# Attention, gated MLP and softplus MLP on one core: Strassen's seven products for the last matrix product of three token groups, and shorter chains of small vector instructions

## The chip, the cores and the metric

The kernel runs on one core of a Trainium2 chip. The metric is the device time of one execution in microseconds (us). Time before: a median of 699.16 us over 3 runs (698.99 to 699.61). The profile that is read below comes from one more execution, which took 698.44 us, with a span of 696.5 us from its first to its last instruction.

## The reference, cut to what matters

```python
# q, k, v: (4, 8, 576, 64) fp32; heads 0-3 see a window of 32 keys, heads 4-7 every 4th key of 128
attn = softmax(where(mask, q @ k.T / 8, -1e9))        # per head
x = (attn @ v) laid out as (2304, 512)                # tokens x (heads * 64)
h = x @ moe_w_in                                      # (2304, 1024)
solu = h * softmax(h)
ln = (solu - mean(solu)) / sqrt(var(solu) + 1e-6) * g_ln
y = ln @ moe_w_out                                    # (2304, 512)
h2 = y @ moe2_w_in                                    # (2304, 2048)
g = maximum(h2, 0) + log1p(exp(-abs(h2)))             # softplus
out = g @ moe2_w_out                                  # (2304, 512) fp32
```

## The kernel before, in words

All matrix products of the MLPs are made with fp16 operands that stand for fp32 ones: each operand is split into a high and a low half (`... h` and `... l` operations: a cast on VectorE or ScalarE, then a subtraction on VectorE), and each product is three matmuls (high by high, high by low, low by high) that add up in PSUM. The weights come in as fp32, are scaled by a power of two that is found on the chip (`weights`: sum of squares on ScalarE, a sum over the partitions by a matmul with a tile of ones, then a chain of small VectorE instructions, `scale_of` and what follows it), and are split into the tile `W`, which holds all four matrices for the rest of the run.

The 2304 tokens go through in 28 attention pairs, 18 tiles of 128 tokens for the first MLP's first product, softmax and norm (`m1`), and 9 groups of 256 tokens, numbered 0 to 8, for everything after that. The norm needs 1/sqrt(var + eps); it is made on VectorE from an integer guess and Newton steps (the chain `m1k`, 9 instructions of one column, and `m1x`).

Of a group, `y` = ln @ w_out comes first, then, for 8 pairs of 128 hidden columns (p = 0 to 7), the hidden product, the softplus on ScalarE (`sp`), the split of its result g into halves (`gh`, `gl`), and the output product (`o`), which adds into the PSUM tile `ps_w`. One `o` of one p is 2 token halves x 2 hidden halves x 3 = 12 matmuls, with g as the stationary operand (128x128) and 512 columns of w2_out moving.

Groups 5 and 6, and 7 and 8, go in twos (`TWINS`, functions `twin_weights`, `y_twin`, `mlp2_twin`): their hidden product is made by Strassen's method in Winograd's form, with seven products of blocks (`P5.0.1` to `P7.3.7`: twin, quarter of the hidden columns, product) in place of eight. That takes sums of weight blocks (`tw..`), sums of y blocks (`yt..`) and sums of the products out of PSUM (`U`, `C`), all on VectorE. The output products `o` are still plain ones in all nine groups.

The order of the work is a list of numbers, `ORDER`: one sequence of operations over all engines, which was found by a search outside the kernel; each engine runs its own operations in that order. For an operation that either VectorE or ScalarE could do, the number also says which one does it. `SLOTS` says which buffer each tile takes. Negative numbers are matmuls without use (`eye` by `eye`, 512 columns), which stand where TensorE was expected to have nothing to do; they are called fillers below. There are 142.

Of the kernel before, what the change touches and what calls it, by code (L numbers as in the profile page):

```python
# [1749 lines left out]
```

## Time and profile before

| what | value |
|---|---|
| median of 3 runs | 699.16 us |
| profiled execution: time, span | 698.44 us, 696.5 us |
| PE (TensorE matmul) busy | 675.2 us, 97% of the span, 5223 records |
| DVE (VectorE) busy | 556.0 us, 80% |
| ACT (ScalarE) busy | 480.9 us, 69%, of which 55.2 us are 43 loads of an activation table |
| DMA moved | 89.8 MB |
| mean granted TensorE clock | 0.988 of full speed |

The busy time of PE includes the fillers, so a busy PE is not yet a useful PE. A matmul's duration in the trace (379 ns for 512 columns) is longer than the distance to the next one, because they overlap in the array; distances between starts tell the rate. VectorE's records overlap a little too. Shares over the whole span mix stages with different limits, so the rows below are read by stage.

### The profile page before, as it was taken

Reading aid. Unit: us, or ns where it says so; the run is one execution under the profiler, and the core shown is the slowest. Engines: PE = TensorE matmul, PEld = TensorE weight load, DVE = VectorE, ACT = ScalarE, POOL = GpSimd, SP = SyncE. Lnnn points to the kernel's source line nnn. Section 1 sums busy time; section 2 is a strip of 40 time slices with the busy share of each in tenths; the row PEclk is TensorE's granted clock in tenths of the full one; section 3 lists DMA queues with packets and bytes.
Section 4 is the critical chain, followed back from the end, with each engine's and each line's share of the span. In section 5 each row is a group of like instructions: output and inputs, shape, how many; then the busy total and the mean of one; then the engine's idle time right before and its main releaser. Section 6 shows DMA issues by size and latency. Waiting matters only on the chain.

```text
span 696.5 us, 14184 instructions
## 1 busy us (share of the span) xinstructions
PE 675.2 (97%) x5223; PEld 463.9 (67%) x5223; DVE 556.0 (80%) x1619; ACT 480.9 (69%) x1015; POOL 3.5 (1%) x22
## 2 busy tenths in 40 slices
PE   7999699999999999999999999999999999999997
PEld 4665547766765588688667668666776668676653
DVE  4999999999999968788889899887887768544233
ACT  4889998999998776987799797976364632322312
POOL 2000000000000000000000000000000000000000
PEclk9999689999999999999999999999999999999999
DMA  9889987669876558989887887652012110000001
GB/s 266 247 233 259 225 225 193 162 170 188 184 147 164 146 176 185 200 162 157 158 152 153 153 162 136 116 113 43 1 31 62 31 31 1 1 32 31 1 1 60
DMA packets 186773, 89.80 MB, mean 129 GB/s; under 512 B 157000, under 2 KB 174416, under 8 KB 186704
## 3 DMA queue, kind: packets, MB, share of 16 engines
...
## 4 chain that ended last, share of the span: by engine, by line
PE 69%; DVE 12%; DMA 10%; ACT 4%; issue 3%; SPq 1%; ACTq 0%; DVEq 0%
PE ps_w L552 31%; PE bank L552 26%; PE bank L1550 11%; DMA xd<-x 2%; DVE E L543 2%; DMA E<-in_v_dram 2%; DMA qT<-qk 1%; DMA pT<-p 1%; DVE W L543 1%; PE bank L558 1%; DVE s L1122 1%; DMA W<-in_moe_w_out_dram 1%; ACT E L534 1%; DMA rv<-in_v_dram 1%; DMA rq<-in_q_dram 1%
## 5 line engine op out<-in xcount | busy, mean ns | idle before, releaser
L552 PE MATMUL ps_w<-W,g 128*128 128x512 f16 x864 | 194.3, 379 | 0.0
L552 PEld LDWEIGHTS <-W 128*128 128x128 f16 x1824 | 176.5, 98 | 23.3 <-DMA lnT<-hl 0.7
L552 PEld LDWEIGHTS <-g 128*128 128x128 f16 x864 | 83.6, 98 | 91.4
L552 PE MATMUL bank<-y,W 128*128 128x256 f16 x960 | 109.9, 273 | 0.0
L552 PE MATMUL ps_w<-W,xr 128*128 128x512 f16 x432 | 99.5, 382 | 1.0 <-ACT xr L534 1.0
L552 PE MATMUL bank<-lnT,W 128*128 128x256 f16 x864 | 98.7, 273 | 0.2 <-DMA lnT<-hl 0.2
L552 PEld LDWEIGHTS <-xr 128*128 128x128 f16 x432 | 42.1, 99 | 46.9 <-ACT xr L534 1.5
L543 DVE SCALAR_TENSOR_TENSOR g<-r,KR,g 128x512 f16<-128x512 f32 x68 | 50.3, 744 | 15.2 <-ACT g L534 14.2
L1718 ACT ACT_TABLE_LOAD x43 | 55.2, 1283 | 0.7
L1550 PEld LDWEIGHTS <-W 128*128 128x128 f16 x480 | 47.0, 98 | 8.4
L534 ACT ACTIVATE E<-E 128x768 f32<-128x768 f32 (+3 forms) x51 | 37.9, 744 | 15.7 <-DVE E L543 8.8
L534 ACT ACTIVATE s<-s 96x128 f32<-96x128 f32 (+3 forms) x144 | 43.5, 374 | 2.4 <-DVE st L538 1.2
L1122 DVE CUSTOM_DVE_ANT_0 s<-bank,band,bsc 96x128 f32<-96x128 f32 (+3 forms) x144 | 38.9, 324 | 3.9 <-PE bank L552 3.6
L534 ACT ACTIVATE r<-bank,invC 128x512 f32<-128x512 f32 x40 | 27.2, 685 | 16.4 <-PE bank L552 15.5
L534 ACT ACTIVATE r<-r,invT 128x512 f32<-128x512 f32 x21 | 14.6, 714 | 32.5 <-DVE r L546 32.4
L534 ACT ACTIVATE xf<-bank,rs 80x64 f32<-80x64 f32 (+1 forms) x128 | 29.3, 314 | 7.2 <-DVE rs L549 4.8
L552 PE MATMUL ps_w<-eye 128*128 128x512 bf16 x108 | 31.4, 407 | 0.7 <-DVE e L543 0.7
L534 ACT ACTIVATE g<-r,KR 128x512 f16<-128x512 f32 x35 | 24.9, 715 | 6.6 <-PE ps_w L552 6.3
L552 PEld LDWEIGHTS <-pT 128*96 128x96 f16 (+3 forms) x432 | 23.1, 123 | 6.9 <-issue 1.5
L543 DVE SCALAR_TENSOR_TENSOR E<-E 128x512 int32<-128x512 int32 x40 | 27.1, 683 | 0.1
L552 PEld LDWEIGHTS <-eye 128*128 128x128 bf16 (+2 forms) x162 | 16.5, 111 | 15.8 <-POOL eye L611 4.0
L534 ACT ACTIVATE hl<-e,st 128x1024 f16<-128x1024 f32 x18 | 22.3, 1242 | 5.4 <-DMA lnT<-hl 3.2
...
## 6 DMA issues: line engine op xcount, KB each, us to landing
...
```

The costliest lines, as they stand in the source:

```text
L534: pin(nc.scalar.activation(out=out, in_=in_, func=func, **kw))
L543: pin(nc.vector.scalar_tensor_tensor(out=out, in0=in0, scalar=s, in1=in1, op0=op0, op1=op1, **kw))
L552: pin(nc.tensor.matmul(out, l, r, start=start, stop=stop))
L558: pin(nc.tensor.transpose(out, in_, eye32[:in_.shape[0], :in_.shape[0]]))
L1122: pin(nc.vector.tensor_tensor_reduce(out=sv()[:rows, h, :nk], in0=sb.t[:rows, h, :nk], in1=band[:rows, 48 - m:48 - m + nk], scale=sc[:rows ...
L1550: pin(nc.tensor.matmul(ps.t[:, ff, :], at(w, cc, ff), yo.t[:, v, cc, :], start=start, stop=cc == 1 and x == 2, skip_group_check=True,))
L1718: pin(nc.scalar.preload_act_table_set(TABLES[tab]))
```

## The change

1. **Output product by Strassen for groups 6, 7 and 8** (`OTW`). For each p the 2x2 blocks (2 token halves x 2 hidden halves by 2 hidden halves x 2 column halves of 256) are multiplied with seven products (`oa`: 1, `ob`: 3, `oc`: 3) in place of eight: 21 matmuls of 256 columns for 12 of 512. It needs, once, sums of blocks of w2_out (`twin_out_weights`, operations `to`), split into halves; for each group and p, four sums of g blocks (`so`, 128 columns each), split into halves (`ho`, `lo`); and at a group's end eight VectorE or ScalarE instructions of 256 columns (`oe`) that add up the products out of PSUM, for two of 512 columns. The split of the plain g is cut from 512 to 384 columns there.
2. **Root chain**: the first two integer steps become one, and two Newton steps with other coefficients stand for three: `m1k` has 7 instructions for 9.
3. **Scale chains**: the sum over partial sums moves from a VectorE reduction to further matmuls with the tile of ones (4 or 8 matmuls of one column for one matmul of 4 or 8; 3 of up to 3 columns for one of up to 9); the reciprocal of a power of two becomes an integer subtraction; some copies fall away.
4. **The third sum of the twin's weights** takes the place of a block of `W` that is no longer needed; several buffers move.
5. **`ORDER` and `SLOTS` are new throughout**: 3046 entries for 2834, with 137 fillers for 142.

```diff
-    def scale_of(inv, sc, ss):
+    def scale_of(inv, sc, ss, uses):
 
         i = sc.bitcast(INT32)
         return [
-            (TINY, lambda e: ts(sc, ss() if callable(ss) else ss, 2.0 ** -80, op0=ALU.max)),
+            (dve_cost(0, x=1), lambda e: ts(sc, ss(), 2.0 ** -80, op0=ALU.max), [], uses),
             (TINY, lambda e: ts(i, i, 24, 23, ALU.logical_shift_right, ALU.logical_shift_left)),
-            (TINY, lambda e: recip(inv, sc)),
-            (TINY, lambda e: ts(inv, inv, 2.0 ** -50)),
+            (TINY, lambda e: ts(inv.bitcast(INT32), i, -1.0, float((254 - 50) << 23), ALU.mult, ALU.add)),
         ]
...
-        m = P.op(f"{name}m", pe_cost(0.15), lambda e: mm(pb.t[:, 0:n], ones, am[:, 0:n], True, True), after=squares, uses=[pb])
+        cols = list(range(n))
+
+        def total(e):
+            for i in cols:
+                mm(pb.t[:, 0:1], ones, am[:, i:i + 1], i == cols[0], i == cols[-1])
+
+        m = P.op(f"{name}m", pe_cost(0.06 + 0.06 * len(cols)), total, after=squares, uses=[pb])
...
-            (TINY, lambda e: pin(nc.vector.tensor_reduce(out=t[:, 0:1], in_=pb.t[:, 0:n], axis=AXX, op=ALU.add)), [], [pb]),
-            *scale_of(inv, sc, t[:, 0:1]),
+            *scale_of(inv, sc, lambda: pb.t[:, 0:1], [pb]),
...
-            lambda e: ts(i32(9), i32(7), 1, op0=ALU.logical_shift_right),
-            lambda e: ts(i32(9), i32(9), -1.0, float(0x5F3759DF - 2 ** 31), ALU.mult, ALU.add),
+            lambda e: ts(i32(9), i32(7), -0.5, float(0x5F3759DF - 2 ** 31), ALU.mult, ALU.add),
...
+    def twin_out_weights(p):
+
+        wt, f = w2o[p // 2], (2 * p) % 4
+        F = [Buf(sf_pool), Buf(sf_pool)]
+        tb = Buf(t2_pool)
+        lo, hi = slice(0, 256), slice(256, 512)
+        o = [
+            P.op(
+                f"to{p}f{i}", dve_cost(512), lambda e, i=i: tt(F[i].t, wt[:, 0, f + i, :], wt[:, 1, f + i, :], ALU.add),
+                after=[*w2_d[p // 2][1]], uses=[F[i]],
+            ) for i in range(2)
+        ]
+        t1 = P.op(f"to{p}t1", dve_cost(256), lambda e: tt(F[0].t[:, lo], F[0].t[:, hi], F[0].t[:, lo], ALU.subtract), after=[o[0]], uses=[F[0]])
...
+        for i, src in enumerate((t3, t4)):
+            at = slice(512 * i, 512 * i + 512)
+            h = P.op(f"to{p}h{i}", either(512), lambda e, i=i, at=at: cast(e, tb.t[0][:, at], F[i].t), after=[src, t2] if i == 0 else [src], uses=[F[i], tb])
+            l = P.op(f"to{p}l{i}", dve_cost(512), lambda e, i=i, at=at: tt(tb.t[1][:, at], F[i].t, tb.t[0][:, at], ALU.subtract), after=[h], uses=[F[i], tb])
...
+    def out_seven(n):
...
+        def step(p, k, rb, gb, split):
...
+            s1 = P.op(f"so{m}.1", cost, lambda e: tt(a22(), a21(), a22(), ALU.add), after=split, uses=[rb])
+            s3 = P.op(f"so{m}.3", cost, lambda e: tt(a21(), a11(), a21(), ALU.subtract), after=[s1], uses=[rb])
+            s2 = P.op(f"so{m}.2", cost, lambda e: tt(a11(), a22(), a11(), ALU.subtract), after=[s3], uses=[rb])
+            s4 = P.op(f"so{m}.4", cost, lambda e: tt(a12(), a12(), a11(), ALU.subtract), after=[s2], uses=[rb])
+            h2 = P.op(f"ho{m}", either(512, ptr=1), lambda e: scaled(e, g2.t[:, 0], rb.t, KR[:, cq]), after=[s4], uses=[rb, g2])
...
+            def products(which, new):
+                for q, gt, ff, t, b, start in which:
+                    start = start and new
+                    for x, (a, w) in enumerate(((0, 0), (0, 1), (1, 0))):
+                        pin(nc.tensor.matmul(
+                            mi[q](), gt.t[:, a, ff, 128 - 128 * t:256 - 128 * t], b(w), start=start and x == 0, stop=x == 2, skip_group_check=True,
+                        ))
...
+        def end():
...
+            m1_ = P.op(f"oe{n}m1", either(256, ptr=1, psum=1), lambda e: scaled(e, ub.t[:, lo], mi[1](), d), after=all_ops["a"], uses=[*both, ub])
+            u2 = plus("u2", lambda: ub.t[:, hi], 6, lambda: ub.t[:, lo], [m1_, *all_ops["b"]], [*both, ub])
```

The new order is seen at three places. First VectorE where the last weight matrix quarter gets its scale (`s2o` is the scale, `bank` the PSUM tile with the sums, `tmp` a scratch column, `invC` the first instruction behind the scale). Before:

```order
L738 TENSOR_REDUCE tmp_90<-bank_137 128x1
L538 TENSOR_SCALAR s2o<-tmp_90 128x1
L540 TENSOR_SCALAR s2o<-s2o 128x1
L549 RECIPROCAL s2o<-s2o 128x1
L538 TENSOR_SCALAR s2o<-s2o 128x1
L543 SCALAR_TENSOR_TENSOR invC<-s2i,s1o 128x1
```

And now, with the three instructions ahead of it:

```order
L1269 TENSOR_REDUCE st_121<-ps_w_141 128x1
L565 RECIPROCAL st_120<-st_120 128x1
L559 SCALAR_TENSOR_TENSOR st_120<-st_120 128x1
L554 TENSOR_SCALAR s2o<-bank_138 128x1
L556 TENSOR_SCALAR s2o<-s2o 128x1 x2
L559 SCALAR_TENSOR_TENSOR invC<-s2i,s1o 128x1
```

Three small instructions stand for five.

Then VectorE a little later, where the root of a tile of 128 tokens is made (`st` holds its columns, `W<-E,s2o` are splits of weights that lie between). Before:

```order
L540 TENSOR_SCALAR st_119<-st_119 128x1
L538 TENSOR_SCALAR st_119<-st_119 128x1
L540 TENSOR_SCALAR st_119<-st_119 128x1
L543 SCALAR_TENSOR_TENSOR st_119<-st_119 128x1 x6
L543 SCALAR_TENSOR_TENSOR W<-E,s2o,W 128x512
L540 TENSOR_SCALAR st_119<-st_119 128x2
```

And now:

```order
L556 TENSOR_SCALAR st_120<-st_120 128x1
L559 SCALAR_TENSOR_TENSOR W<-E,s2o,W 128x512
L556 TENSOR_SCALAR st_120<-st_120 128x1
L559 SCALAR_TENSOR_TENSOR st_120<-st_120 128x1 x5
L556 TENSOR_SCALAR st_120<-st_120 128x2
```

Seven instructions of one column stand for nine ahead of the one of two columns.

Last VectorE at the end of the run (`r`, `e`, `hl`, `E`, `W` hold softplus results, `g` their split halves, `osb` the output, `ps_w` the output sums in PSUM; now `s`, `v`, `p` hold the split sums). Before:

```order
L543 SCALAR_TENSOR_TENSOR g_129<-r_128,KR,g_129 128x512
L546 TENSOR_TENSOR r_127<-bank_137,osb_134 128x512
L538 TENSOR_SCALAR g_131<-r_126,KR 128x512
L543 SCALAR_TENSOR_TENSOR g_130<-e_117,KR,g_130 128x512
L543 SCALAR_TENSOR_TENSOR g_131<-r_126,KR,g_131 128x512
L543 SCALAR_TENSOR_TENSOR g_129<-r_125,KR,g_129 128x512
L546 TENSOR_TENSOR r_126<-bank_137,osb_135 128x512
L543 SCALAR_TENSOR_TENSOR g_131<-hl,KR,g_131 128x512
L538 TENSOR_SCALAR g_130<-r_126,KR 128x512
L538 TENSOR_SCALAR osb_133<-ps_w_141,iD 128x512
```

And now:

```order
L559 SCALAR_TENSOR_TENSOR g_130<-hl,KR,g_130 128x384
L562 TENSOR_TENSOR e_118<-e_118 128x128
L559 SCALAR_TENSOR_TENSOR s_114<-r_126,KR,s_114 128x512
L562 TENSOR_TENSOR e_118<-e_118 128x128
L562 TENSOR_TENSOR hl<-hl 128x128 x3
L559 SCALAR_TENSOR_TENSOR v_112<-e_118,KR,v_112 128x512
L562 TENSOR_TENSOR hl<-hl 128x128
L559 SCALAR_TENSOR_TENSOR g_131<-r_129,KR,g_131 128x384
L562 TENSOR_TENSOR r_129<-r_129 128x128
L559 SCALAR_TENSOR_TENSOR s_113<-hl,KR,s_113 128x512
L562 TENSOR_TENSOR r_129<-r_129 128x128 x2
L559 SCALAR_TENSOR_TENSOR g_132<-r_127,KR,g_132 128x384
```

Where VectorE had one or two instructions for each p, it now has six, and the sums of neighbouring steps are laid into each other. Counted over the order from the first seven-product step of groups 5 and 6 (`P5.0.1`) to the end, VectorE has 413 operations for 214; up to the last sum over the partitions (that of the last quarter of w2_out) it has 541 for 580.

## Rows read from the trace of the kernel before

**Rows 1.** First part of the page: busy us of each engine, share, instructions.
```profile
PE 675.2 (97%) x5223; PEld 463.9 (67%) x5223; DVE 556.0 (80%) x1619; ACT 480.9 (69%) x1015; POOL 3.5 (1%) x22
```

**Rows 2.** Busy time by stretch: PE, weight loads, DVE, ACT, POOL; granted clock, DMA.
```profile
0.00:50.00 50.00, 45.79 (x355) 29.66 (x356) 39.63 (x99) 36.60 (x116) 3.54 (x22) 1.00 0.92 250
50.00:236.00 186.00, 175.94 (x1330) 117.61 (x1329) 180.33 (x548) 167.94 (x403) 0.00 (x0) 0.95 0.78 189
236.00:494.00 258.00, 255.48 (x2189) 184.30 (x2187) 218.67 (x759) 204.69 (x394) 0.00 (x0) 1.00 0.72 144
494.00:692.00 198.00, 197.96 (x1356) 132.37 (x1353) 116.66 (x216) 70.98 (x103) 0.00 (x0) 1.00 0.09 22
692.00:696.50 4.50, 0.00 (x0) 0.00 (x0) 0.75 (x1) 0.69 (x1) 0.00 (x0) 1.00 0.31 117
```

**Rows 3.** The fillers: matmul groups that read only eye, whole run.
```profile
L552 PE MATMUL ps_w<-eye 128*128 128x512 bf16 x108 | 31.4, 407 | 0.7 <-DVE e L543 0.7
...
L552 PE MATMUL bank<-eye 128*128 128x512 bf16 x34 | 10.8, 421 | 4.9 <-POOL eye L611 4.0 <-ACT qk L534 0.9
```

**Rows 4.** Timeline of PE around the last fillers: start us, us, instruction.
```profile
234.79 1.03 PE L552 MATMUL bank<-eye 128*128 128x512 bf16 x4
235.66 2.75 PE L552 MATMUL ps_w<-W,xr 128*128 128x512 f16 x12
238.25 0.28 PE L552 MATMUL bank<-amw,ones 128*128 128x4 f32 x2
238.39 2.75 PE L552 MATMUL ps_w<-W,xr 128*128 128x512 f16 x12
```

**Rows 5.** Waits of PE from 236 us to the end: first and last of 4.
```profile
PE bank L552 <- DMA pT<-p: 1.0, 1, 1.0
...
PE bank L552 <- ACT xf L534: 0.4, 1, 0.4
```

**Rows 6.** Timeline of PE near the end: hidden products (bank) and output products (ps_w).
```profile
641.12 1.47 PE L1550 MATMUL bank<-y,W 128*128 128x256 f16 x12
642.43 1.47 PE L1550 MATMUL bank<-kT,W 128*128 128x256 f16 x12
...
646.36 2.75 PE L552 MATMUL ps_w<-W,g 128*128 128x512 f16 x12
648.95 1.47 PE L1550 MATMUL bank<-y,W 128*128 128x256 f16 x12
```

**Rows 7.** Weight loads from 550 to 690 us, largest group.
```profile
L1550 PEld LDWEIGHTS <-W 128*128 128x128 f16 x396 | 38.8, 98 | 7.0
```

**Rows 8.** DVE groups by form from 494 us to the end.
```profile
L543 DVE SCALAR_TENSOR_TENSOR g<-r,KR,g 128x512 f16<-128x512 f32 x29 | 21.5, 747 | 14.3 <-ACT g L534 13.8
L546 DVE TENSOR_TENSOR osb<-bank,osb 128x512 f32<-128x512 f32 x16 | 11.0, 689 | 14.1 <-PE bank L1550 13.9
...
L538 DVE TENSOR_SCALAR g<-r,KR 128x512 f16<-128x512 f32 x16 | 7.7, 483 | 10.9 <-PE ps_w L552 10.1 <-issue 0.4 <-ACT r L534 0.3
```

**Rows 9.** DVE by form, whole run: two-operand instruction of 256 columns.
```profile
L546 DVE TENSOR_TENSOR xf<-bank,rs 96x256 f32<-96x256 f32 x9 | 3.8, 417 | 0.2
```

**Rows 10.** Timeline of DVE: two independent instructions near the end.
```profile
684.66 1.42 DVE L543 SCALAR_TENSOR_TENSOR g<-r,KR,g 128x512 f16<-128x512 f32 x2
```

**Rows 11.** Timeline of DVE in the last scale chain and a root chain.
```profile
238.76 0.15 DVE L538 TENSOR_SCALAR s2o<-tmp 128x1 f32<-128x1 f32 x1
238.95 0.15 DVE L540 TENSOR_SCALAR s2o<-s2o 128x1 int32<-128x1 int32 x1
239.14 0.16 DVE L549 RECIPROCAL s2o<-s2o 128x1 f32<-128x1 f32 x1
```

**Rows 12.** Timeline of PE early on: fp32 matmuls (passes) in a row.
```profile
17.00 1.30 PE L552 MATMUL bank<-xd,pT 80*80 80x65 f32 x16
```

**Rows 13.** Timeline of all engines from 686 us to the end.
```profile
685.75 6.21 PE L552 MATMUL ps_w<-W,g 128*128 128x512 f16 x28
...
692.04 0.69 ACT L534 ACTIVATE osb<-ps_w,iD 128x512 f32<-128x512 f32 x1 [8.95 <-issue]
692.75 1.12 SPq L561 DMA_DIRECT2D out_dram<-osb  x2
692.76 0.75 DVE L538 TENSOR_SCALAR osb<-ps_w,iD 128x512 f32<-128x512 f32 x1 [6.69 <-ACT osb L534]
```

**Rows 14.** Waits of all engines from 494 to 692 us: the hand-overs of g.
```profile
DVE g L543 <- ACT g L534: 22.1, 7, 8.3
```

More of the change, by code (lines that the diff above doesn't have):

```diff
@@ L423 @@
     iD = mem([128, 1], FP32, "iD")
+    niD = mem([128, 1], FP32, "niD")
     KR0 = mem([128, NQ], FP32, "KR0")
@@ L1355, in y_stage @@
             y_ops[j] += [yh, yl]
+    plain_h = [[] for _ in range(NQ)]
     def mlp2(j):
@@ L1519, in y_twin, with plus @@
         split("t4", b21, [t4])
         return ops
+    def out_seven(n):
+        if not to_done:
+            for p in range(NP):
+                twin_out_weights(p)
+        pa, pb = Buf(ps_w), Buf(ps_w)
+        mi = (None, lambda: pa.t[:, 0, 0:256], lambda: pa.t[:, 0, 256:512], lambda: pb.t[:, 1, 0:256], lambda: pb.t[:, 0, 0:256],
+              lambda: pa.t[:, 1, 0:256], lambda: pa.t[:, 1, 256:512], lambda: pb.t[:, 0, 256:512])
+        firsts = {}
+        all_ops = {x: [] for x in "abc"}
+        def step(p, k, rb, gb, split):
+            wt, f = w2o[p // 2], (2 * p) % 4
+            tb, td = to_done[p]
+            g2 = Buf(gq_pool)
+            c = p // 2
+            cq = slice(c, c + 1)
+            a11, a12, a21, a22 = (lambda ff=ff, t=t: rb.t[:, ff, 128 * t:128 * t + 128] for t in (1, 0) for ff in range(2))
+            m = f"{n}.{p}"
+            cost = dve_cost(128)
+            s1 = P.op(f"so{m}.1", cost, lambda e: tt(a22(), a21(), a22(), ALU.add), after=split, uses=[rb])
[3 more added lines that the diff above has]
+            h2 = P.op(f"ho{m}", either(512, ptr=1), lambda e: scaled(e, g2.t[:, 0], rb.t, KR[:, cq]), after=[s4], uses=[rb, g2])
+            l2 = P.op(
+                f"lo{m}", dve_cost(512, x=1), lambda e: stt(g2.t[:, 1], rb.t, KR[:, cq], g2.t[:, 0], ALU.mult, ALU.subtract), after=[h2], uses=[rb, g2],
+            )
+            plain = lambda ff, dh: (lambda w: wt[:, w, f + ff, 256 * dh:256 * dh + 256])
+            summed = lambda i: (lambda w: tb.t[w][:, 256 * i:256 * i + 256])
+            def products(which, new):
[5 more added lines that the diff above has]
+                        ))
+            now = {x: x not in firsts for x in "abc"}
+            parts = {
+                "a": ((1, gb, 0, 0, plain(0, 0), True),),
+                "b": ((5, g2, 1, 1, summed(0), True), (6, g2, 0, 0, summed(3), False), (7, g2, 0, 1, summed(1), True)),
+                "c": ((2, gb, 1, 0, plain(1, 0), False), (4, gb, 1, 1, summed(2), False), (3, g2, 1, 0, plain(1, 1), True)),
+            }
+            ready = {"a": split, "b": [h2, l2], "c": [*split, h2, l2]}
+            for x, which in parts.items():
+                used = [pa, pb, *([gb] if x != "b" else []), *([g2] if x != "a" else []), *([tb] if x != "a" else [])]
+                o = P.op(
+                    f"o{x}{m}", pe_cost(0.109 * 3 * len(which)), lambda e, which=which, new=now[x]: products(which, new), cols=0.768 * len(which),
+                    after=[*ready[x], *w2_d[c][1], *(td if x != "a" else []), *firsts.values()], uses=used,
+                )
+                firsts.setdefault(x, o)
+                all_ops[x].append(o)
+        def end():
+            o1, o2, ub = Buf(osb_pool), Buf(osb_pool), Buf(ue_pool)
+            lo, hi = slice(0, 256), slice(256, 512)
+            cost = dve_cost(256, x=1)
+            d = iD[:, 0:1]
+            def plus(name, out, q, in1, after, uses, by=d):
+                return P.op(f"oe{n}{name}", cost, lambda e: stt(out(), mi[q](), by, in1(), ALU.mult, ALU.add), after=after, uses=uses)
+            both = [pa, pb]
+            m1_ = P.op(f"oe{n}m1", either(256, ptr=1, psum=1), lambda e: scaled(e, ub.t[:, lo], mi[1](), d), after=all_ops["a"], uses=[*both, ub])
+            u2 = plus("u2", lambda: ub.t[:, hi], 6, lambda: ub.t[:, lo], [m1_, *all_ops["b"]], [*both, ub])
+            u3 = plus("u3", lambda: o2.t[:, lo], 7, lambda: ub.t[:, hi], [u2], [*both, ub, o2])
+            u4 = plus("u4", lambda: o1.t[:, hi], 5, lambda: ub.t[:, hi], [u2], [*both, ub, o1])
+            c11 = plus("c11", lambda: o1.t[:, lo], 2, lambda: ub.t[:, lo], [m1_, *all_ops["c"]], [*both, ub, o1])
+            c22 = plus("c22", lambda: o2.t[:, hi], 5, lambda: o2.t[:, lo], [u3], [*both, o2])
+            c12 = plus("c12", lambda: o1.t[:, hi], 3, lambda: o1.t[:, hi], [u4, *all_ops["c"]], [*both, o1])
+            c21 = plus("c21", lambda: o2.t[:, lo], 4, lambda: o2.t[:, lo], [u3, c22, *all_ops["c"]], [*both, o2], niD[:, 0:1])
+            for ti, (ob, w) in enumerate(((o2, [c21, c22]), (o1, [c11, c12]))):
+                r0 = n * GRP + ti * 128
+                P.op(f"out{n}.{ti}", dma_cost(0.5, 2.0), lambda e, r0=r0, ob=ob: dma(out[r0:r0 + 128, :], ob.t), after=w, uses=[ob], mv=moving(128, 2048))
+        return step, end
@@ L1522, in mlp2_twin, with split @@
     def mlp2_twin(j, ops):
-        po = [Buf(ps_w), Buf(ps_w)]
+        po = [None if j + th in OTW else Buf(ps_w) for th in range(2)]
         o_prev = [None, None]
+        later = [[], []]
+        seven = [out_seven(j + th) if j + th in OTW else None for th in range(2)]
+        def split(name, rb, gb, cq, after, c0=0):
+            part = lambda t: t.rearrange("p f c -> p (f c)")[:, c0:]
+            gh = P.op(f"gh{name}", either(512 - c0, ptr=1), lambda e: scaled(e, part(gb.t[:, 0]), part(rb.t), KR[:, cq]), after=after, uses=[rb, gb])
+            gl = P.op(
+                f"gl{name}", dve_cost(512 - c0, x=1), lambda e: stt(part(gb.t[:, 1]), part(rb.t), KR[:, cq], part(gb.t[:, 0]), ALU.mult, ALU.subtract),
+                after=[gh], uses=[rb, gb],
+            )
+            return [gh, gl]
@@ L1578, in unit @@
                 )
-                gh = P.op(f"gh{n}.{k}", either(512, ptr=1), lambda e, rb=rb, gb=gb, cq=cq: scaled(e, gb.t[:, 0], rb.t, KR[:, cq]), after=[sp], uses=[rb, gb])
-                gl = P.op(
-                    f"gl{n}.{k}", dve_cost(512, x=1),
-                    lambda e, rb=rb, gb=gb, cq=cq: stt(gb.t[:, 1], rb.t, KR[:, cq], gb.t[:, 0], ALU.mult, ALU.subtract), after=[gh], uses=[rb, gb],
-                )
+                if seven[th] is not None:
+                    later[th].append((f"{n}.{k}", 2 * qd + fh, k, rb, cq, sp))
+                    continue
+                gb = Buf(g_pool)
+                gh, gl = split(f"{n}.{k}", rb, gb, cq, [sp])
                 first = o_prev[th] is None
@@ L1598, in mlp2_twin @@
         for th in range(2):
+            if seven[th] is not None:
+                step, end = seven[th]
+                for name, p, k, rb, cq, sp in later[th]:
+                    gb = Buf(go_pool)
+                    step(p, k, rb, gb, split(name, rb, gb, cq, [sp], 128))
+                end()
+                continue
             for ti in range(2):
@@ L1694 @@
         u_pool.add(t, opens=early_osb)
-    parts = lambda t: t.bitcast(FP16).rearrange("p (k a f c) -> p k a f c", k=4, a=2, f=2)
+    parts = lambda t: t.bitcast(FP16).rearrange("p (k a f c) -> p k a f c", k=3, a=2, f=2)
     for i in range(2):
-        tw_pool.add(parts(E[:, 2048 * i:2048 * (i + 1)]), opens=att, until=2)
+        tw_pool.add(parts(E[:, 1536 * i:1536 * (i + 1)]), opens=att, until=2)
     for i in range(2):
-        tw_pool.add(parts(WF[:, 2048 * i:2048 * (i + 1)]), opens=m1_all, since=2)
+        tw_pool.add(parts(WF[:, 1536 * i:1536 * (i + 1)]), opens=m1_all, since=2)
     e_mem = e_pool.slots[0][0]
-    for t in (e_mem, hl_mem):
-        for i in range(2):
-            r_pool.add(two(t[:, 512 * i:512 * (i + 1)]), opens=m1_all)
+    for i in (6, 7):
+        r_pool.add(two(cut(E, i)), opens=att)
+    for t in (cut(e_mem, 0), cut(e_mem, 1), cut(hl_mem, 0), cut(hl_mem, 1), cut(WF, 7)):
+        r_pool.add(two(t), opens=m1_all)
+    both = lambda a, b: (a.bitcast(FP16), b.bitcast(FP16))
+    for i in range(2):
+        t2_pool.add(both(cut(xr_mem, 2 * i), cut(xr_mem, 2 * i + 1)), opens=m1_all)
+    for i in range(4):
+        t2_pool.add(both(cut(WF, 8 + 2 * i), cut(WF, 9 + 2 * i)), opens=y_all)
+    for i in range(2):
+        t2_pool.add(both(cut(ln_mem, 2 * i), cut(ln_mem, 2 * i + 1)), opens=y_all)
+    for i in (10, 11, 12):
+        gq_pool.add(slots[i].bitcast(FP16).rearrange("p (a f c) -> p a f c", a=2, f=2), opens=yf_all)
+    ue_pool.add(slots[13], opens=yf_all)
+    g_all = [u for x in g_pool.bufs for u in x.users]
+    for x in g_pool.slots:
+        go_pool.add(x[0], opens=g_all, place=x[4])
     for p in (qk_pool, qT_pool, kT_pool, pT_pool, xd_pool):
```

84 lines of the change are left out of this document (51 added, 33 removed), and 368 rows, old and new, of tables (ORDER, SLOTS).

## The prediction

> **What bounds the kernel now.** I read the page's first part, then a table of stretches, then what PE waits for. PE is busy 97% of the span and DVE 80% [rows 1], but by stretch the picture changes [rows 2]. The first 50 us start empty and are full of transfers. From 50 to 236 us DVE is busy 180.33 of 186 us: it converts, scales and splits the weights, and PE, busy 175.94, is partly busy with fillers. The 142 fillers take 42.2 us of PE's records [rows 3], and the last four stand at 234.79 us [rows 4]. From 236 us on PE is the limit: 255.48 of 258 us, then 197.96 of 198. Four waits are all that PE has from there to the end, the longest 1.0 us [rows 5]. In the last stretch, which begins with the first seven-product step at 494 us, DVE has 116.66 us of work and 81 us of leisure [rows 2]. So work taken from PE behind 236 us shortens the run directly, as long as DVE keeps up; work taken from DVE helps only ahead of 236 us.
>
> **Output product: what PE gains.** Starts show the rate [rows 6]: twelve matmuls of 256 columns take 642.43 - 641.12 = 1.31 us (0.109 each), twelve of 512 take 648.95 - 646.36 = 2.59 (0.216 each). One step becomes 21 x 0.109 = 2.29 us for 2.59, and 24 steps (3 groups x 8) save 24 x 0.297 = 7.1 us. Each matmul has its own weight load, as now; one takes 98 ns [rows 7], under 109, so it stays hidden. All 24 steps lie in the last stretch: PE's 198.0 us become 190.9.
>
> The row on 256 columns can be set against a rule that speaks against this change: the Trainium skill, "TensorEngine Tiling (Array Packing)", section "Instruction Overhead", gives each matmul about 60 cycles on top of its columns. By that rule 12 x 572 and 21 x 316 cycles at 2.4 GHz are 2.86 and 2.77 us, a saving of 24 x 0.095 = 2.3 us in place of 7.1. The trace disagrees: 256 columns take 0.109 us where the rule makes 0.132.
>
> **What DVE pays for it.** In the last stretch, by the order, these are new. An instruction that doesn't need the one before it starts 0.08 us before that one's end (two of 0.747 take 1.42 [rows 10]); one that does starts 0.04 after it (0.15 long, 0.19 apart [rows 11]). Two-operand instructions take 0.689 us for 512 columns [rows 8] and 0.417 for 256 [rows 9], hence by the slope about 0.28 for 128.
> - 96 `so` of 128 columns, 40 of them right behind the one that they need: 40 x 0.32 + 56 x 0.20 = 24.0.
> - 24 `lo` of 512 at 0.747 - 0.08: 16.1.
> - `to`, once: 32 of 512 at 0.61 and 32 of 256 at 0.34: 30.4.
> - 23 `oe` of 256 from PSUM, at 0.747 less 256 columns' slope, some 0.40 apart: 9.2.
> - 6 casts and scalings at 0.40 and 11 more twin operations at about 0.5: 7.9.
> - Less: 13 `gh` that go to ACT (0.40 each, from 0.483 [rows 8]), 4 `oe` of 512, 2 `U`, 128 columns in each of 24 `gl`, 6 of the m1 chains: 14.1.
>
> That is 73.5 us more: 116.7 + 73.5 = 190.2 us of DVE work beside 190.9 us of PE work. The cover that hid DVE's work is used up. The fullest that DVE was in any long stretch is 180.33 of 186, 97% [rows 2]; at that share 190.2 us need 196.1. So the last stretch lies between 190.9 (DVE never late) and 196.1. I take 195.0, nearer the second, because the last operations hang on each other across DVE, ACT and PE: **-3.0 us**. ACT gains 21 `ho` and 13 casts of some 0.7, 24 us on 71 of 198: no limit.
>
> **Sums over partitions.** The last weight sum now takes 0.14 us of PE (238.25 to 238.39 [rows 4]), two fp32 passes. Four matmuls make eight passes; passes in a row are about 0.07 us apart for 80 rows ((1.30 - 0.24) / 15 [rows 12]), for 128 rows perhaps 0.1. That is +0.4 to +0.7 for it and +0.3 to +0.5 for each of two batch sums behind it: 1.3 us. Two fillers now stand behind that sum: 0.4. Together **+1.7 us** on PE's path.
>
> **Front.** Up to the last weight sum DVE has 541 operations for 580, nearly all of the missing ones with one column: 35 of them (12 of root chains, 23 of scale chains and copies) at 0.08 (spacing when independent) to 0.19 [rows 11] are 2.8 to 6.6 us. Where DVE is 97% busy that comes back in time. Against it, the sum matmuls make each of ten weight chains start later: about 0.3 to 0.7 us for four partial sums, while two instructions fewer give back 0.38; if all eight chains of the second MLP lay on the path and the sums cost the most, that is 8 x 0.32 = +2.6 us. The new order has 7 fillers fewer ahead of that sum, 7 x 0.216 = 1.5 us. From +2.6 to -6.6 I take **-3.0**, between the fillers and the instructions. Shorter root chains behind 236 us cost or give nothing: PE's other work covers them.
>
> **End.** Today ACT and then DVE empty PSUM one after the other, 0.69 and 0.75 us [rows 13]. In the new one `u2`, `u3`, `u4`, `c22` fit beside PE's last two operations (1.9 us), and three instructions of some 0.4 to 0.5 follow. I count **0**; bounds -0.3 and +0.8.
>
> **Sum.** -3.0 + 1.7 - 3.0 + 0 = -4.3 us on the profiled execution's 698.44: 694.1. The median of the runs is 0.72 above that execution, so 694.9 us.
>
> **Rivals.**
> - *DVE never late.* The interleaving in the order is dense enough. Then the last stretch is 190.9: 4.1 us less, 690.8 us, and with the whole 6.6 in front 687.2. For it: now PE hasn't one wait in 198 us. Against it: DVE has nothing left.
> - *The saving is eaten.* DVE's chains stretch the last stretch to its 198 us of today (share 96%), or the front is lost to the longer sums: 694.9 + 3.0 = 697.9, up to 700.5 with a front at its worst. Time as before. For it: DVE at 190.2 of 198 with hand-overs.
> - *Slower: DVE and ACT pass g to and fro.* In each of 24 steps g goes ACT (`gh`), DVE (`gl`, four sums), ACT (`ho`), DVE (`lo`), so 48 hand-overs from ACT to DVE. Now seven such waits cost 22.1 us [rows 14], though at leisure. If each costs more than 0.22 us that other work doesn't fill, the stretch passes 200.7 and the kernel is slower by over 0.2%; at 0.3 us it is 190.2 + 14.4 = 204.6, and the time 704.5.
> - *256-column matmuls at 0.132 us* (the page's rule above). PE would need 198.0 - 2.3 = 195.7 and the time would be 695.6 at the least. The rows on such matmuls exclude it all but entirely.
>
> **How the numbers follow.** Likeliest, 0.47: DVE nearly full, 694.9 (692 to 698). DVE never late: 0.20. Saving eaten: 0.19. Slower: 0.12. The page's rule: 0.02. The range 688.5 to 701.0 leaves out the best of the second case and most of the fourth. A difference of 0.2%, 1.4 us, is about what a measurement of this kernel tells from none. Faster: 0.43 of the first case, 0.20, 0.06 of the third, 0.02, together 0.71. Same: 0.04 + 0.11 + 0.02 = 0.17. Slower: 0.02 + 0.10 = 0.12.
>
> **What would show it.** PE's new matmuls of 256 columns 0.109 us apart, 24 x 21 of them. DVE busy over 93% from the first seven-product step to PE's end, and that stretch 193 to 197 us long, with a few us of PE waits, most of them on g or its sums; none means the second case, over 10 us the fourth. The last filler about 3 us earlier than 235.8. The sum matmuls 0.07 to 0.1 us apart per pass. The prediction is wrong if PE waits in the last stretch for something else (a transfer, a buffer), or if the front is not ruled by DVE's work at all, so that its 39 operations bring nothing.

## The result: 706.0 us, slower by 1%

The changed kernel takes 706.0 us (median of 4 runs, 704.5 to 708.9), the kernel before beside it 699.1: ratio 1.0105, 95% interval 1.0071 to 1.0138. The forecast was 694.9 and its range ended at 701.0. The profiled execution took 705.7 us with a span of 704.0.

The busy line of the page after, which answers to [rows 1]; DVE has 63 us more work in all, PE 4 more:
```profile
PE 679.1 (96%) x5526; PEld 496.6 (71%) x5526; DVE 619.4 (88%) x1762; ACT 497.7 (71%) x1005; POOL 3.5 (1%) x22
```

Busy time by stretch after, cut at the same events as [rows 2] (50 us, last weight sum, first seven-product step, PE's end):
```profile
0.00:50.00 50.00, 41.09 (x333) 28.35 (x334) 30.70 (x78) 31.32 (x102) 3.52 (x22) 1.00 0.94 223
50.00:248.00 198.00, 191.40 (x1436) 130.25 (x1434) 188.12 (x532) 172.85 (x402) 0.00 (x0) 0.95 0.74 184
248.00:503.50 255.50, 254.42 (x2180) 183.30 (x2179) 215.94 (x743) 196.97 (x357) 0.00 (x0) 1.00 0.73 146
503.50:698.50 195.00, 192.17 (x1586) 154.71 (x1583) 182.21 (x407) 96.54 (x146) 0.00 (x0) 1.00 0.09 23
698.50:704.00 5.50, 0.00 (x0) 0.00 (x0) 2.47 (x6) 0.00 (x0) 0.00 (x0) 0.72 0.25 95
```
The last stretch is 195.0 us, as forecast (198.2 before). The loss is in front: DVE is busy 30.70 of the first 50 us for 39.63 [rows 2], and the last weight sum starts at 248.0 us for 238.3 [rows 4]. The granted clock between 50 us and that sum is 0.95 in both kernels, so the clock isn't the difference.

PE's timeline after, at that sum; it answers to [rows 4]:
```profile
247.98 0.95 PE L568 MATMUL bank<-amw,ones 128*128 128x1 f32 x8
248.79 2.75 PE L568 MATMUL ps_w<-W,xr 128*128 128x512 f16 x12
251.37 0.59 PE L568 MATMUL bank<-eye 128*128 128x512 bf16 x2
```
One sum is eight passes in 0.95 us where it was two in 0.28. Over the whole run, the largest groups of PE that sum over partitions, after and then before:
```profile
L568 PE MATMUL bank<-amw,ones 128*128 128x1 f32 x96 | 12.1, 244 | 1.7 <-ACT E L550 1.1 <-ACT W L550 0.3
L568 PE MATMUL bank<-am,ones 128*128 128x3 f32 x18 | 2.3, 242 | 0.3 <-DVE s2o L554 0.3
```
```profile
L552 PE MATMUL bank<-amw,ones 128*128 128x4 f32 x16 | 2.9, 252 | 0.8 <-ACT W L534 0.6 <-ACT E L534 0.2
L552 PE MATMUL bank<-amw,ones 128*128 128x8 f32 x4 | 0.6, 225 | 0.0
```
With the smaller groups it is 120 passes for 28, and the record of a pass is about as long for one column (244 ns) as for four (252) or eight (225).

The start of DVE's timeline after:
```profile
5.73 0.49 DVE L586 COPY kT<-bank 128x320 f32<-128x320 f32 x1 [4.67 <-PE bank L574]
6.14 0.48 DVE L554 TENSOR_SCALAR qT<-bank 128x320 f32<-128x320 f32 x1
9.35 0.49 DVE L586 COPY qk<-bank 128x320 f32<-128x320 f32 x1 [2.73 <-PE bank L574]
11.17 0.89 DVE L1034 TENSOR_REDUCE s<-bank 80x4 f32<-80x320 f32 x2 [1.32 <-PE bank L568]
...
14.03 0.48 DVE L586 COPY pT<-bank 80x320 f32<-80x320 f32 x1 [1.76 <-PE bank L574]
16.07 0.16 DVE L554 TENSOR_SCALAR tmp<-bank 128x1 f32<-128x1 f32 x1 [1.56 <-PE bank L568]
...
18.26 0.41 DVE L556 TENSOR_SCALAR W<-E 128x512 int32<-128x512 int32 x1
```
and of SP's queue after, then before:
```profile
8.89 0.95 SPq L577 DMA_DIRECT2D rk<-in_k_dram  x2
10.36 0.99 SPq L577 DMA_DIRECT2D E<-in_moe_w_in_dram  x2
```
```profile
3.70 0.83 SPq L561 DMA_DIRECT2D E<-in_moe_w_in_dram  x2
```
The first pieces of the first weight matrix are asked for 6.7 us later, and their first conversion (W<-E, int32) stands at 18.26 us; before it stood at 8.96, between the attention's first steps, where DVE now waits 2.73, 1.32, 1.76 and 1.56 us for PE.

By stage, on the profiled executions (spans 696.5 and 704.0): front +9.7 us, from the last weight sum to the first seven-product step (called the middle below) 0.0, last stretch -3.2, end +1.0. (Expectations below that give 248.3 us for this kernel's last weight sum mean its third pass; its start is 248.0.)

### The profile page after: what moved, and what is told of

The parts are those of the page before. It is cut to its first block, busy times and chain, and to the rows that moved or that the text cites. A ratio compares the mean times of both kernels' runs of the same rounds, so it can differ in the third digit from the quotient of the medians.

```text
span 704.0 us, 14948 instructions
## 1 busy us (share of the span) xinstructions
PE 679.1 (96%) x5526; PEld 496.6 (71%) x5526; DVE 619.4 (88%) x1762; ACT 497.7 (71%) x1005; POOL 3.5 (1%) x22
## 4 chain that ended last, share of the span: by engine, by line
PE 59%; DVE 21%; ACT 8%; DMA 7%; issue 3%; SPq 1%; DVEq 0%; ACTq 0%
PE bank L568 23%; PE ps_w L568 20%; PE ps_w L1612 7%; PE bank L1696 7%; PE bank L574 2%; DMA rq<-in_q_dram 2%; ACT e L550 2%; DVE s L1143 2%; DVE hl L562 1%; DVE g L559 1%; ACT hl L550 1%; ACT s L550 1%; DMA pT<-p 1%; DVE e L559 1%; DVE kT L562 1%
## 5 line engine op out<-in xcount | busy, mean ns | idle before, releaser
L568 PEld LDWEIGHTS <-W 128*128 128x128 f16 x1824 | 177.3, 98 | 25.4 <-issue 1.2
L568 PE MATMUL ps_w<-W,g 128*128 128x512 f16 x576 | 130.4, 379 | 0.0
L568 PEld LDWEIGHTS <-g 128*128 128x128 f16 x576 | 55.1, 98 | 59.9 <-DVE g L559 0.2
L1696 PEld LDWEIGHTS <-W 128*128 128x128 f16 x528 | 51.6, 98 | 8.1 <-issue 1.0
L550 ACT ACTIVATE g<-r,KR 128x512 f16<-128x512 f32 (+1 forms) x46 | 31.5, 689 | 18.8 <-PE ps_w L568 10.4
L559 DVE SCALAR_TENSOR_TENSOR g<-r,KR,g 128x512 f16<-128x512 f32 (+1 forms) x56 | 40.0, 717 | 3.0 <-ACT g L550 2.8
L550 ACT ACTIVATE r<-bank,invC 128x512 f32<-128x512 f32 x40 | 27.1, 683 | 10.3 <-PE bank L568 10.1
L568 PE MATMUL ps_w<-eye 128*128 128x512 bf16 x106 | 29.2, 389 | 0.0
L1612 PE MATMUL ps_w<-W,g 128*128 128x256 f16 x180 | 26.3, 272 | 1.3 <-DVE osb L559 1.0
L562 DVE TENSOR_TENSOR p<-s,p 96x512 f16<-96x512 f32 (+3 forms) x36 | 21.9, 608 | 5.0 <-ACT p L550 4.7
L550 ACT ACTIVATE e<-ps_w,st,bsc 128x1024 f32<-128x1024 f32 x16 | 19.3, 1206 | 7.9 <-DVE st L554 7.8
```

The costliest lines, as they stand in the source:

```text
L550: pin(nc.scalar.activation(out=out, in_=in_, func=func, **kw))
L559: pin(nc.vector.scalar_tensor_tensor(out=out, in0=in0, scalar=s, in1=in1, op0=op0, op1=op1, **kw))
L562: pin(nc.vector.tensor_tensor(out=out, in0=a, in1=b, op=op))
L568: pin(nc.tensor.matmul(out, l, r, start=start, stop=stop))
L1612: pin(nc.tensor.matmul(mi[q](), gt.t[:, a, ff, 128 - 128 * t:256 - 128 * t], b(w), start=start and x == 0, stop=x == 2, skip_group_check=True,
L1696: pin(nc.tensor.matmul(ps.t[:, ff, :], at(w, cc, ff), yo.t[:, v, cc, :], start=start, stop=cc == 1 and x == 2, skip_group_check=True,))
```

## The experiments

Two theories on the front: **T1**, the new sequence loses it, by the late transfers; **T2**, the longer sums lose it. **T3**: the seven products cost it elsewhere. The kernels have the changed kernel's code with one part or the other put back, and a sequence made of the two sequences' pieces: up to the last weight sum that of before ("old") or of the change ("new"), and behind it the new one unless the text says otherwise.

**Four runs with a fault of mine.** They were to tell T1 from T2, but their fillers went to the first free bank, not to the one that the sequence names. PE's order, chains_alone (-) and chains_alone_2 (+):
```diff
- L547 MATMUL bank_137<-eye 128x512
+ L547 MATMUL ps_w_141<-eye 128x512
```


> The changed kernel with every edit in it, but with the sequence of the kernel before (transfers, conversions, fillers and all) up to the last weight sum, and the new sequence behind it. Theory T1, the new sequence loses the 10 us in front: the last weight sum comes back from 248.3 us to about 238 (235 to 239), the tail stays at 195.0 us, and the time is 694 to 698. Theory T2, the longer sums and changed chains lose it wherever they stand: the last weight sum stays behind 245 us and the time is 702 to 706. Theory T3, the seven products of the second product cost it through buffers or ACT: the time stays near 706.

713.3 us (1.0215, 1.018 to 1.025).

> The kernel before in its own sequence throughout, with only the shorter root and scale chains and their longer sums in it, and without the seven products of the second product. T1: 697 to 700, with the last weight sum at 235 to 240 us. T2: 705 or more, with the last weight sum at 245 us or later. The prediction's own front term alone (-3.0, and +1.7 behind it) would give about 698.

711.9 us (1.0177, 1.0152 to 1.0203).

> Without the seven products of the second product: the new sequence up to the last weight sum, and the sequence of the kernel before behind it; the shorter chains are in it. T1: the front is late as in the changed kernel (last weight sum at about 248 us), the tail is 198 us, and the time is 709 (707 to 711). T3, and any theory that puts the loss on the new tail's work: 699 to 701.

723.0 us (1.036, 1.0327 to 1.0394).

> The changed kernel with the sequence of the kernel before up to the sum of the first weight matrix alone (32.7 us there, 41.6 in the changed kernel), and the new sequence behind it. T1 in its narrow form, the late loads of the first weight matrix leave DVE idle in the first 45 us and nothing gives that back: the sum of the first matrix is at 33 us, the last weight sum at about 240 and the time 697 (695 to 699). T1 in its wide form, the new sequence loses all along the front: the lead of 9 us at the first sum melts away, the last weight sum is at 244 to 248 us and the time 702 to 706.

716.1 us (1.0257, 1.0235 to 1.0279).

Three are slower than any theory says; the time of chains_alone, by itself, would fit T2. But the groups of fillers in chains_alone show another reason, and the other three have it too:
```profile
L547 PE MATMUL bank<-eye 128*128 128x512 bf16 x129 | 38.8, 415 | 14.1 <-POOL eye L605 4.0 <-ACT pT L529 2.7 <-ACT kT L529 2.2
L547 PE MATMUL ps_w<-eye 128*128 128x512 bf16 x13 | 3.6, 379 | 0.0
```
Before, 108 fillers write ps_w [rows 3]; here 129 write small banks, and PE stands 14.1 us ahead of them (4.9 before), among other things until ACT has read the bank. These runs say nothing on T1 and T2.

**The same with the fillers in their own banks**, and two more that put the old chains back in the changed kernel:
```diff
-                mm(pb.t[:, 0:1], ones, am[:, i:i + 1], i == cols[0], i == cols[-1])
...
+        m = P.op(f"{name}m", pe_cost(0.15), lambda e: mm(pb.t[:, 0:n], ones, am[:, 0:n], True, True), after=squares, uses=[pb])
```


> As chains_alone, but each filler writes to the same bank as in the kernel before. In the first four runs the fillers of the front went to the first free bank of the small ones, and PE stood there until ACT or DVE had read it; so those four tell nothing of T1 against T2 until that is taken out. T1 (the loss of the changed kernel is its new sequence): 697 to 701, last weight sum at 235 to 240 us. T2 (the longer sums and the chains behind them): 705 to 710, last weight sum at 245 us or later. T4, the fillers' banks alone made these runs late: the time falls by 10 us or more from the 711.9 of chains_alone.

> As old_front, each filler in the bank that the sequence before gave it: the changed kernel with all its edits, in the sequence of the kernel before up to the last weight sum. T1: 694 to 698 (699 less the 3 us of the tail), last weight sum at about 238 us. T2: 702 to 707.

> The seven products of the second product alone: root, scale and sum chains as in the kernel before, its sequence up to the last weight sum, the new one behind it. T1 and T2 both: the front is untouched, the last weight sum at 238 us, the tail at 195.0, the time 694 to 698. T3 (the seven products cost it): 703 or more.

> The new sequence throughout, with the seven products, but root, scale and sum chains as in the kernel before (one matmul for each sum over partitions, then a reduction; 75 short DVE instructions more, each right behind the one that it follows). T1: 704 to 709, last weight sum at about 248 us. T2: 694 to 699, last weight sum at 236 to 240 us.

| | ratio to before (95%) | last weight sum | to first seven-product step | last stretch |
|---|---|---|---|---|
| before | 1 | 238.3 | 255.5 | 198.2 |
| chains_alone_2 | 1.0049 (1.0033 to 1.0064) | 240.9 | 255.4 | 198.2 |
| old_front_2 | 1.0069 (1.0044 to 1.0093) | 241.9 | 258.3 | 195.2 |
| seven_alone | 1.0006 (0.9988 to 1.0024) | 237.8 | 257.8 | 197.0 |
| new_sequence_old_chains | 1.0115 (1.0059 to 1.0170) | 244.2 | 257.4 | 196.7 |
| changed kernel | 1.0105 (1.0071 to 1.0138) | 248.0 | 255.5 | 195.0 |

The medians of the four are 701.5, 702.7, 699.3 and 706.7 us. The other columns are from one profiled execution each, and such a column scatters: four executions of one and the same front (one_sum, one_sum_again, one_sum_late_cut and short_sums_tail, below) put the last weight sum at 237.4, 238.0, 237.9 and 234.9 us. So a difference of under 3 us between two rows counts only where the ratios bear it out. T4 holds: chains_alone_2 takes 701.5 us where chains_alone took 711.9. Neither T1 nor T2 holds alone: with the old sequence the chains put the last weight sum 2.7 us later (chains_alone_2 against before) or 4.0 (old_front_2 against seven_alone), with the old chains the new sequence puts it 6.4 later, and both together make the 9.7. T3 falls for the front. Seven_alone, forecast at 694 to 698 us, shows besides that the seven products without the short chains gain nothing.

**Sums or chains?** one_sum keeps the short root and scale chains, but makes each sum one matmul and one reduction on DVE; one_sum_late_cut has the old sequence up to the first seven-product step. The other two look for the place of the sequence's loss, with old chains.
```diff
-            for x in range(3):
-                mm(pb.t[:, c0:3], ones, am[:, 3 * c0 + x:9:3], x == 0, x == 3 - 1)
+        m = P.op(f"pre{b}m", pe_cost(0.15), lambda e: mm(pb.t[:, 3 * c0:9], ones, am[:, 3 * c0:9], True, True), after=parts, uses=[pb])
...
+            (TINY, lambda e: pin(nc.vector.tensor_reduce(out=t[:, 0:1], in_=pb.t[:, 0:n], axis=AXX, op=ALU.add)), [], [pb]),
```


> Old sequence up to the last weight sum, the new one behind it, seven products, short root and scale chains, but each sum over partitions again as one matmul and one reduction on DVE. T2s (what the chains cost is their many short passes on PE and DVE's wait for them: 120 passes and 15.1 us of PE records against 28 and 4.6): last weight sum at 235 to 238.5 us, time 696 to 699. T2c (fewer instructions in the chains bring nothing, or the other edits of the chains cost): 240 to 242 us, 700 to 703.

695.99 us, ratio 0.9980 (0.9968 to 0.9991), last weight sum at 237.4: T2s. Against old_front_2, which differs in the sums alone, it is 4.5 us ahead at the last weight sum, and its ratio is lower by 0.9%, some 6 us. It beats both kernels.

> As one_sum, but with the sequence of the kernel before up to the first seven-product step (P5.0.1, 493.8 us there). T5, the 2.2 us that seven_alone loses between the last weight sum and that step come from the new sequence's middle: the step comes at 490 to 493 us, the tail is 195 to 197, the time 692 to 696. If the middle lost because of work moved ahead of the tail, the tail gives it back: 198 us or more, time 696 to 700.

700.7 us (1.0042, 1.0028 to 1.0056): the step at 494.0, the stretch behind it 198.5. T5 falls: from the last weight sum to the step it is 256.2 us with the old middle and 256.3 in one_sum with the new, so the old middle saves nothing. Nor does the 198.5 show that work was moved, for PE waits 5.37 us right behind the place where the two sequences join:
```profile
500.88 4.41 PE L565 MATMUL bank<-y,W 128*128 128x256 f16 x24 [5.37 <-DVE p L551]
```

> The new sequence with the chains of the kernel before (as new_sequence_old_chains, 706.7 us, last weight sum at 244.3), but with the sequence of the kernel before up to the sum of the first weight matrix (32.6 us). T1 narrow (the 6 us that the sequence loses in front are the late loads of the first matrix): last weight sum at 238 to 240 us, time 699 to 702. T1 wide (the sequence goes on losing behind 40 us): last weight sum at 242 to 245 us, time 704 to 708.

704.2 us (1.0094, 1.0074 to 1.0113), last weight sum at 242.7.

> The same with the sequence of the kernel before up to the sum of the weights w2i1 (116.5 us). T1, narrow or wide up to there: last weight sum at 237 to 240 us, time 699 to 702. If the loss stands behind 117 us: 242 us or more, 704 or more.

707.6 us (1.0154, 1.0129 to 1.0180), last weight sum at 245.7. Here too time is lost where the two sequences join: in old_first_117 DVE is busy 2.88 us between 120 and 130. As cuts these two tell nothing sure.

**Where the sequence loses.** DVE's busy time tells it without cuts. From windows of each run, idle is length less busy time:

| us | DVE idle 0 to 40 | DVE busy to last weight sum | idle behind 40 | last weight sum |
|---|---|---|---|---|
| before | 10.1 | 222.0 | 6.1 | 238.3 |
| seven_alone | 10.0 | 222.1 | 5.7 | 237.8 |
| one_sum | 10.2 | 219.8 | 7.3 | 237.4 |
| old_front_2 | 11.9 | 219.4 | 10.5 | 241.9 |
| chains_alone_2 | 12.3 | 219.2 | 9.4 | 240.9 |
| late_loads | 14.1 | 222.2 | 5.4 | 241.7 |
| after_one_sum | 15.2 | 219.8 | 6.0 | 241.1 |
| new_sequence_old_chains | 15.4 | 223.0 | 5.8 | 244.2 |
| changed kernel | 17.4 | 218.8 | 11.8 | 248.0 |
| early_loads | 18.6 | 222.7 | 3.6 | 244.9 |
| early_loads_and_conversions | 20.7 | 222.8 | 5.0 | 248.5 |

Behind 40 us DVE is idle 4 to 8 us, whatever the sequence, and 9 to 12 with the long sums. What it doesn't do ahead of 40 us mostly stays lost. Three of these rows are runs that moved transfers in SP's queue. late_loads, against before (in early_loads the two transfers move the other way in the new queue, ahead of six others, so that they are the eighth and ninth):
```diff
- DMA E<-in_moe_w_in_dram 128x1024 x2
  DMA W<-in_v_dram 128x768 x2
  DMA xd<-in_v_dram 80x4x128
  DMA qk<-in_v_dram 80x4x128
+ DMA E<-in_moe_w_in_dram 128x1024 x2
```


> The kernel before (697.2 to 699.1 us) with one change: its two first transfers of the first weight matrix stand four places later in SP's queue, behind the attention's. T1 narrow: DVE loses 2 to 5 us ahead of 20 us and doesn't make them up, last weight sum at 240 to 243 us, time 700 to 704. If idle time of DVE in front is made up from its leisure: 238 us, 697 to 699.5.

701.9 us (1.0071, 1.0047 to 1.0095): DVE 4.0 us more idle ahead of 40 us, the last weight sum 3.5 later. One move of two transfers in the old queue costs about half of the 6.4 us that the new sequence costs there.

> new_sequence_old_chains (706.7 us, last weight sum at 244.3 us, DVE 5.4 us behind seven_alone at 40 us) with one change: the two first transfers of the first weight matrix stand five places earlier in SP's queue, their conversions on DVE where they were. If the transfers' arrival is what DVE waits for: DVE is 2 to 3 us less behind, last weight sum at 241 to 243 us, 703 to 705. If the conversions' place in DVE's own order is it: no change, 244 us and 706 to 708.

707.7 us (1.0151, 1.0123 to 1.0178).

> As early_loads, and the six conversions of these two pieces stand on DVE between the first steps of the attention, where DVE waits in the new sequence. T1 narrow (what DVE doesn't do in the first 20 us never comes back): DVE is about 2.5 us less behind at 20 us and at 200 us, last weight sum at 241 to 243 us, time 703 to 705. T1 wide (the lead melts away): ahead at 20 us, but the last weight sum at 244 us and 706 to 708.

707.7 us (1.0150, 1.0092 to 1.0208). Neither remedy helps: the attention's transfers come later instead, and DVE is idle 18.6 and 20.7 us ahead of 40 for 15.4 (in the second of them the granted clock of these 40 us is 0.87 besides, where every other row of the table has 1.00). My narrow cause, that these two transfers come too late, isn't shown for the new sequence; what is shown is that most of the time that DVE waits in its first 40 us is paid at the last weight sum.

**Undoing the sums in the changed kernel itself**, in its own sequence, with one_sum again beside it:

> The changed kernel in its own sequence with one part undone: each sum over partitions is one matmul and one reduction on DVE again. If the two losses add up (6 us for the sums, 6 for the sequence): last weight sum at 241 to 244 us for 248.3, time 699 to 703 for 706.0. If the new sequence hides the sums: 247 to 249 us, 704 to 707.

700.7 us (1.0038, 1.0016 to 1.0059), last weight sum at 241.1 for 248.0: the two losses add up. Which is the larger isn't clear: at the last weight sum the long sums cost 6.9 us, by the ratios (1.0105 to 1.0038) some 4.7; the new sequence costs 3.1 there (238.0 to 241.1) and 5.4 in the medians (695.4 to 700.7).

> one_sum once more, on the chip of after_one_sum: 694.5 to 697, below the kernel before by 0.1 to 0.4%, last weight sum at 235 to 238.5 us.

695.4 us (0.9962, 0.9941 to 0.9983), last weight sum at 238.0.

**What stretches the last stretch?**
```diff
-            s1 = P.op(f"so{m}.1", cost, lambda e: tt(a22(), a21(), a22(), ALU.add), after=split, uses=[rb])
+            s1 = P.op(f"so{m}.1", cost, lambda e: tt(a22()[:, 0:16], a21()[:, 0:16], a22()[:, 0:16], ALU.add), after=split, uses=[rb])
```


> one_sum (696.0 us), but the 96 sums of g's quarters on DVE (so) work on 16 of their 128 columns, so that the last group's outputs are not those of the reference; nothing else is taken away. DVE has about 7 to 10 us less work behind the first seven-product step. If DVE's work is what stretches that stretch from PE's 190.9 to 195.2 us: 192 to 194 us there, 692.5 to 695. If it is hand-overs or the order alone: 195 us, 695.5 to 696.5.

693.2 us (0.9949, 0.9930 to 0.9969; the second measurement of one_sum, 0.9962, lies within that). The last stretch of one_sum, and then of this run:
```profile
493.70:688.90 195.20, 192.31 (x1586) 154.76 (x1584) 182.13 (x407) 96.53 (x146) 0.00 (x0) 1.00 0.09 23
```
```profile
490.70:685.30 194.60, 192.14 (x1586) 154.81 (x1583) 172.84 (x407) 95.95 (x146) 0.00 (x0) 1.00 0.09 23
```
DVE has 9.3 us less to do and the stretch is 0.6 us shorter. So it isn't the amount of DVE's work that stretches it; PE still waits 2.4 us, for the same buffers as in one_sum (2.9). Its span is 3.6 us shorter than one_sum's; 3.0 of these lie ahead of 491 us, where the two kernels are alike, and aren't explained.

## Why the prediction was wrong, step by step

**Output product, right.** PE's timeline after, in the last stretch (it answers to [rows 6]):
```profile
655.03 0.49 PE L1612 MATMUL ps_w<-xr,g 128*128 128x256 f16 x3
655.36 0.49 PE L1612 MATMUL ps_w<-W,v 128*128 128x256 f16 x3
...
657.65 1.47 PE L1612 MATMUL ps_w<-W,s 128*128 128x256 f16 x12
658.96 1.47 PE L1696 MATMUL bank<-y,W 128*128 128x256 f16 x12
```
Three take 0.33 us and twelve 1.31: 0.109 each, as forecast. The rule in the Trainium skill, "TensorEngine Tiling (Array Packing)", section "Instruction Overhead", that each matmul pays some 60 cycles besides its columns, would make them 0.132, an estimate; this trace disagrees, and the fourth rival falls with it.

**What DVE pays: number right, reason wrong.** The stretch came out at 195.0 us, -3.2 where -3.0 stood. DVE is busy 182.2 of it, 93.4%; I had counted 190.2, 8 us too many. But short_sums_tail takes 9.3 us from DVE there and the stretch stays. PE's waits in it, all of them, answer to [rows 5]:
```profile
PE ps_w L1612 <- DVE osb L559: 1.0, 1, 1.0
PE bank L1696 <- DVE osb L562: 0.6, 1, 0.6
PE ps_w L1612 <- ACT p L550: 0.6, 1, 0.6
PE ps_w L1612 <- DVE v L559: 0.3, 1, 0.3
PE ps_w L1612 <- DVE p L554: 0.2, 1, 0.2
```
Five waits, 2.7 us, beside 192.2 us of PE's work: 2.4 for an output buffer or a partial result of the output (osb, and p, which here isn't a sum of g), 0.3 for a sum of g (v). A wait for a buffer was one of my signs that the prediction is wrong. My second reason, the last operations hang on each other, fits in part: 0.5 us of the waits stand in the last 5 us (v and the last p), but 1.5 at 672 to 677 us, in the handing over of ps_w from one group to the next. The share of 97% doesn't fit, and with it as the reason the 195.0 was luck.

**Sums behind 236 us: too dear.** +1.7 stood, 0.0 came. A pass was priced about right: 16 in 1.84 us in the first matrix's sum, (1.84 - 0.24) / 15 = 0.107 apart, for 0.07 to 0.1. What I left out is that shorter root and scale chains help there: from seven_alone to one_sum the middle falls from 257.8 to 256.3 and the last stretch from 197.0 to 195.2 (one execution each; one_sum_again has 256.1 and 195.2). "Cost or give nothing" was wrong. The long sums then cost 2.0 us in the middle behind the old front (old_front_2, 258.3) and nothing in the new sequence throughout (after_one_sum 255.9, changed kernel 255.5): there PE is busy 1.2 us more (253.1 to 254.3), but it waits less, for the transfers pT<-p 0.6 us where after_one_sum has 2.7.

**Front: the step that failed.** -3.0 stood, +9.7 came, and its upper bound was +2.6. In the new sequence the runs part the 9.7: with the old chains the last weight sum is at 244.22 us (+5.97, new_sequence_old_chains), with the short chains and one-matmul sums at 241.07 (-3.15, after_one_sum), with the long sums at 247.98 (+6.91); the ratios of the three, 1.0115, 1.0038 and 1.0105, go the same way. The saving, then, was priced right: DVE's work falls by 3.2 us there (223.0 to 219.8, within the 2.8 to 6.6) and comes back whole. (In the old sequence this isn't clear: of 2.2 us less work 0.2 to 0.9 come back in one_sum and its repetition, 3.3 in short_sums_tail.) Two terms failed. First, the sums: I priced ten chains with four partial sums each, and let eight of them cost 0.32 us. The first two have eight partial sums, 1.84 us for 0.28, and the price isn't that of the chain alone, since DVE stands at the scale chain's first instruction and nothing behind it goes ahead. The timeline after, at the first matrix's sum:
```profile
41.61 1.84 PE L568 MATMUL bank<-amw,ones 128*128 128x1 f32 x16
...
43.48 0.16 DVE L554 TENSOR_SCALAR s1i<-bank 128x1 f32<-128x1 f32 x1 [1.68 <-PE bank L568]
```
The same sum before:
```profile
32.66 0.28 PE L552 MATMUL bank<-amw,ones 128*128 128x8 f32 x2
```
In the old sequence the long sums cost 4.5 us in front, in the new one 6.9. Most of it is what DVE waits for the weight sums (tile amw), in old_front_2 and then in one_sum:
```profile
  DVE s2o L551: 1.7, 2
  DVE s1i L551: 1.6, 1
  DVE s1o L551: 1.5, 1
  DVE s2i L551: 0.8, 2
```
```profile
  DVE tmp L748: 1.3, 3
```
That is 5.6 us for 1.3, or 4.3 of the 4.5; in the changed kernel it is 3.7 (s1i 1.7, s2o 1.1, s2i 0.5, s1o 0.4), and after_one_sum has no such wait. Second, the sequence, which had no term: I looked at how many instructions DVE has and at fillers, not at which transfers SP issues first and what DVE does while the attention starts. That costs 3.1 to 3.7 us with one-matmul sums (one_sum_again 238.0 and one_sum 237.4 to after_one_sum 241.1) and 6.4 with the old chains.

**End: 0 stood, +1.0 came.** PE's last matmul ends 5.6 us ahead of the span's end, before 4.5. The timeline after, for [rows 13]:
```profile
697.95 0.49 PE L1612 MATMUL ps_w<-W,s 128*128 128x256 f16 x3
698.35 0.88 DVE L559 SCALAR_TENSOR_TENSOR osb<-ps_w,iD,p 128x256 f32<-128x256 f32 x2
699.26 0.48 DVE L559 SCALAR_TENSOR_TENSOR osb<-ps_w,iD,osb 128x256 f32<-128x256 f32 x1
699.78 0.48 DVE L559 SCALAR_TENSOR_TENSOR osb<-ps_w,niD,osb 128x256 f32<-128x256 f32 x1
700.18 0.47 DVE L559 SCALAR_TENSOR_TENSOR osb<-ps_w,iD,p 128x256 f32<-128x256 f32 x1
700.57 0.47 DVE L559 SCALAR_TENSOR_TENSOR osb<-ps_w,iD,osb 128x256 f32<-128x256 f32 x1
```
Behind PE's end six combinations follow on DVE, one after the other, where I had counted three: DVE ends 2.6 us behind PE, before 1.6.

**The rivals.** The slower case had the right sign by the wrong mechanism. The waits of DVE for ACT's g, 22.1 us before [rows 14], are gone; for ACT as a whole DVE waits 6.4 us in the last stretch (e 3.3, hl 2.0, s 1.1), and this is the longest:
```profile
DVE e L559 <- ACT e L550: 3.3, 1, 3.3
```
"The front is lost to the longer sums" stood inside the second rival, sized at 2.6 us for what is 4.5 to 6.9 at the last weight sum.

**Still open:** which of the new sequence's moves in the first 40 us make DVE wait (the two that I tried to take back only moved the wait), and the 2.4 us by which short_sums_tail's front is ahead of one_sum's.
